# A third score tile shared by turns with pairs of row maxima, in the last four units of an attention block

## The chip, the cores and the metric

One core of one Trainium2 chip runs the whole kernel as one program. The metric is the time of one execution on the device in microseconds (us), median of several runs; a separate, profiled execution gives the trace.

## What is computed

An adaptive-LayerNorm transformer block on 2048 tokens of 448 channels: attention of 16 heads of 28 channels, and an MLP of 1792 hidden channels.

```python
mod = (_silu(c) @ w_mod).reshape(c.shape[0], 6, 1, -1)
sa, ca, ga, sb, cb, gb = (mod[:, 0], ...)
h = _layernorm(x) * (1 + ca) + sa
x = x + ga * _A_ref(h, A_wqkv, A_wo)    # softmax(q k^T / sqrt(28)) v, 16 heads, then @ wo
h = _layernorm(x) * (1 + cb) + sb
x = x + gb * _B_ref(h, B_w1, B_b1, B_w2, B_b2)   # layernorm, gelu(h @ w1 + b1) @ w2 + b2
```

## The kernel before

The program has three parts: LayerNorm, q, k and v projections with a first share of the row maxima (to 169 us), attention (169 to 831 us), and the MLP (831 us to the end).

**Attention** runs 16 *units* u = 4 g + qt, g a group of four heads and qt a block of 512 queries. A unit has 16 *steps* kt, one for each 128 keys, so there are 256 steps; step = 16 u + kt. A step computes the scores of four heads in two *halves* hf of two heads each. A half is a PSUM tile of two banks, 128 keys x (2 x 512) queries, filled by six matmuls: three terms (high and low parts of q and k) for each of its two heads (L1162). Each head sits in its own 32 rows of the array, half 0 in rows 0 to 63 and half 1 in rows 64 to 127. ACT takes exp of each half (L1167, into slots d and c), and TensorE then multiplies the exps of the step *before* with v (`av`, L1132, four matmuls, the "AV" of a step) into tile o. PE's program is thus: first half, second half, AV of the step before, next step.

**Row maxima.** The softmax needs the maximum of every row of scores before a unit begins; it enters the scores as one more row of q. So beside its own work each step computes some of the maxima of later units: one maximum is one matmul of 28 rows x 512 keys from tiles kh and qh into a bank (L466, `max_mm`) and one VectorE reduce of that bank (L471). They are taken from a queue `mxq`; `n_maxima` gives three or four a step. `emit_max` puts one or two behind the first terms of the first half, and the others behind the last term of the second half. `max_fin` reduces, transposes and writes them into q by DMAs (L502, L509, L512).

**PSUM** has eight banks. Tiles s0 and s1 (two banks each) take the two halves by turns, o one, m1 one, and m2 two buffers of one bank each; maxima go into m1, m2, m2 by turns. When no maximum is left (`three`, in unit 14), `third_tile` closes m2 and opens a third score tile s2 in its banks.

**Units' ends.** When AV of a unit's last step has been issued, in the first step of the next unit, `end_unit` copies o (ACT, L1101) and schedules tasks by steps from there: `t_den` (step + 0, SP DMA L880), `t_rec` (+ 1 where the projection follows: DVE reciprocal, SP DMAs L888 and L890), `t_split` (+ 4, GpSimd L895), `t_split2` (+ 5: DVE cast L905, GpSimd L906). Results of head groups 0 to 2 lie in DRAM. Where the group is the last one, `load_o` (L868, in step + 0, behind `t_den` on SP) loads them, four or six DMAs of 256 KB, and `t_wo(t)` in steps 8 to 11 of units 12 to 15 multiplies them with wo: the *projection steps*. Each has 9 or 12 matmuls L386 into a maximum's bank, an ACT copy L926 and a GpSimd add.

**LayerNorm 2 of the first 512 tokens** starts within attention: 14 stages on VectorE and GpSimd, one a step from `last0 - 12` (last0 = 240, unit 15's first step), and four chunks, one a step from last0 + 3. A chunk has four transposes L267 into a maximum's bank, an ACT cast L994, and a DVE subtract L996 (L998) that frees the bank.

Of the kernel before, what the change touches and what calls it, by code (L numbers as in the profile page):

```python
# [31 lines left out]
NTT = S // 128  # L32
P1RATE = 4
YTAGS = [f"{a}{i}" for a in ("kh", "qh") for i in range(4)]
EPS = 1e-5
# [4 lines left out]
def tile_adaln_block(ctx: ExitStack, tc: tile.TileContext, x, wqkv, wo, w1, b1, w2, b2, c, w_mod, out):  # L40
# [29 lines left out]
    def nm(t):  # L70
        uid[0] += 1
        return f"{t}_{uid[0]}"
# [10 lines left out]
    def slot4(tag, inner, dt=F32R):  # L83
# [4 lines left out]
        return lambda k: t2[k // 2][:, k % 2]  # L88

    def ps_s2():  # L90
        s_ring.append(s_ring.pop(0))
        key = s_ring[-1]
        return ps_pools[key][1].tile([128, 2, 512], F32, tag=key, name=nm(key), bufs=1)

# [380 lines left out]
    def pair_diff(g, qt, i, j):  # L475
# [12 lines left out]
        return rest  # L488

    def load_hi(kind, g, b):  # L490
        tg = ("kh" if kind else "qh") + str(b)
# [70 lines left out]

    last_j = [None]

    def emit_max(n, half=None):
        for _ in range(n):
            if not mxq:
                return
            fits = [x for x, m in enumerate(mxq[:32]) if half is None or (m[4] // 2 == half and m[4] != last_j[0])]
            g, qt, cch, i, j = mxq.pop(fits[0] if fits else 0)  # L570
            last_j[0] = j
            max_one(g, qt, cch, i, j)
            count(g, qt, [cch])


# [219 lines left out]
    for key in ("s0", "s1"):  # L795
        ps_open(key)
    s_ring[:] = ["s1", "s0"]
    mx_ring[:] = ["m1", "m2", "m2"]

    def third_tile(on):  # L800
        ps_close("m2" if on else "s2")
        ps_open("s2" if on else "m2", "right")
        s_ring[:] = s_ring + ["s2"] if on else ["s1", "s0"]
        mx_ring[:] = ["m1"] if on else ["m1", "m2", "m2"]

    phase1[0] = False
# [64 lines left out]
    def unit_end_tasks(u, o_sb):  # L871
# [184 lines left out]
    def at(step, fn):  # L1056
        sched.setdefault(step, []).append(fn)
# [49 lines left out]
    o = None  # L1107
    plain = [0]
    three = False


    def is_wo(s_):
        return s_ // NKT >= NU - NB and 8 <= s_ % NKT < 12

    def left_steps(s_):
        rest = range(s_, NKT * (NU - 1) - 6)
        n_wo = sum(is_wo(x) for x in rest)
        return len(rest) - n_wo, n_wo


    def n_maxima(s_):
        n_plain, n_wo = left_steps(s_)
        over = len(mxq) - 7 * n_plain // 2
        if is_wo(s_):
            return max(0, -(-over // max(n_wo, 1)))
        plain[0] += 1
        return 4 if plain[0] % 2 or (over > 3 * n_wo and over > 0) else 3

# [8 lines left out]
    ptags = (["d0", "c0", "c1"], ["c0h", "c1h"])  # L1137
    done_max = set()
    for u in range(NU):
        g, qt = divmod(u, NB)  # L1140
        for kt in range(NKT):
            step = u * NKT + kt
            if kt == 1 and u + 1 < NU and u + 1 not in qst:
                load_q(u + 1)
            if kt == NKT - 6 and u + 1 < NU:
                finish_max(*divmod(u + 1, NB))
            tick_late()
            if not (three or mxq or late):
                three = True
                third_tile(True)  # L1150
            pt = [slot(tags[step % len(tags)], [128, 2, 512], F32) for tags in ptags]
            n = n_maxima(step)
            n0 = 1 if n == 3 and step % 4 == 3 else 2

            ks, qs = kst[(g, kt // 4)], qst[u]
            kc = slice((kt % 4) * 128, (kt % 4 + 1) * 128)
            for hf in range(2):
                s2 = ps_s2()
                for term, (kp, qp) in enumerate(((0, 0), (1, 0), (0, 1))):
                    for jj in range(2):  # L1160
                        rows_ = slice(64 * hf + 32 * jj, 64 * hf + 32 * jj + DH + (term == 0))
                        pe.matmul(s2[:, jj, :], ks[rows_, kp, kc], qs[rows_, qp, :], start=(term == 0), stop=(term == 2))  # L1162
# [4 lines left out]
                act.activation(pt[hf], s2, AF.Exp, scale=SCALE)  # L1167
# [22 lines left out]


    third_tile(False)
    w_copy[0] = act.copy
    LAG = 2
# [102 lines left out]
```

## Time and profile before

| what | value |
|---|---|
| median of 3 runs | 1128.87 us (1128.83 to 1129.13) |
| profiled execution | 1130.08 us, span 1128.0 us |
| TensorE (PE) busy | 1116.4 us, 99% of the span |
| VectorE (DVE) | 843.7 us, 75% |
| ScalarE (ACT) | 672.0 us, 60% |
| GpSimd (POOL) | 209.6 us, 19% |
| granted TensorE clock | full in all 40 slices |
| DMA | 81.19 MB, 72 GB/s in the mean |

A matmul's end is modelled in the trace, its start is recorded. A step's length is therefore read from the start of its first score matmul to that of the next step. A row of the timeline has start, duration, engine, line, operation, tiles and, in brackets, the idle time of the engine ahead of it and what ended it.

### The profile page before, as it was taken

The page shows a single profiled execution, that of the slowest core. Times are in us where ns is not written, and L with a number is a line of the kernel's source. Part 1 is how long each engine was busy: PE and PEld are TensorE (multiplying, and loading weights), DVE is VectorE, ACT ScalarE, POOL GpSimd, SP SyncE. Part 2 cuts the span into 40 slices and gives each one's busy share as a digit, 9 for nine tenths or more (in the row PEclk, how much of TensorE's full clock was granted, in tenths as well). Part 3 has the DMA queues.
Part 4 walks back from the last instruction along what each step waited for, and adds up shares of the span by engine and source line. Part 5 has one row for each costly group of instructions (what it writes and reads, how often), then busy time and mean ns, then how long its engine had stood idle before and what let it go on. Part 6 is the DMA issues. An engine that isn't in the chain of part 4 may idle for free.

```text
span 1128.0 us, 20665 instructions
## 1 busy us (share of the span) xinstructions
PE 1116.4 (99%) x8319; PEld 670.1 (59%) x8319; DVE 843.7 (75%) x1485; ACT 672.0 (60%) x823; POOL 209.6 (19%) x211
## 2 busy tenths in 40 slices
PE   8999999999999999999999999999999999999998
PEld 6756674444444444444444454545468888888887
DVE  6968788999999999999999978595448853444322
ACT  4555657888887888788788867576752321111110
POOL 1533332110000000000000020217114504123000
PEclk9999999999999999999999999999999999999999
DMA  9562263121121211311111312020422100000000
GB/s 303 202 200 88 91 200 114 48 84 41 58 95 57 58 40 57 91 53 58 53 44 58 112 41 83 4 85 1 137 73 78 35 33 1 1 33 1 33 1 33
DMA packets 49341, 81.19 MB, mean 72 GB/s; under 512 B 12311, under 2 KB 18702, under 8 KB 49234
## 3 DMA queue, kind: packets, MB, share of 16 engines
q1 hardware_dynamic: 48762, 79.14, 22.1%
q8 instruction: 65, 1.06, 0.4%
q10 hardware_dynamic: 148, 0.46, 0.1%
q0 software_dynamic: 336, 0.28, 0.1%
q14 instruction: 30, 0.25, 0.1%
HBM read 55.04 MB, written 26.48 MB: 72 GB/s over the span
## 4 chain that ended last, share of the span: by engine, by line
PE 94%; DVE 3%; ACT 1%; DMA 1%; issue 1%; POOL 0%; SPq 0%; DVEq 0%; ACTq 0%; POOLq 0%
PE s L1162 26%; PE o L1132 22%; PE m L386 16%; PE pa L386 8%; PE m L466 6%; PE s L1232 3%; PE s L1233 3%; PE s L1231 3%; DVE mxp L471 2%; PE t L1232 1%; PE t L1233 1%; PE t L1231 1%; DMA slot_c<-in_w_mod_dram 1%; PE ma L466 1%; PE o L267 1%
## 5 line engine op out<-in xcount | busy, mean ns | idle before, releaser
L471 DVE TENSOR_REDUCE mxp<-m 128x1 f32<-128x512 f32 x884 | 568.8, 686 | 75.3 <-PE m L466 41.1
L1162 PE MATMUL s<-slot_b,slot_a 28*128 28x512 f32 (+1 forms) x3072 | 376.3, 420 | 0.0
L1162 PEld LDWEIGHTS s<-slot_b,slot_a 28*128 28x128 f32 (+1 forms) x3072 | 213.0, 184 | 247.4 <-ACT slot_c L1167 124.1
L466 PE MATMUL m<-kh,qh 28*128 28x512 f32 x863 | 287.6, 472 | 1.2 <-DVE mxp L471 0.9
L1167 ACT ACTIVATE slot_c<-s 128x1024 f32<-128x1024 f32 x170 | 174.3, 1025 | 75.9 <-PE s L1162 75.6
L1132 PE MATMUL o<-slot_c,v 128*32 128x512 f32 x680 | 178.8, 605 | 0.0
L1208 ACT ACTIVATE full<-m,b_col 128x512 f32<-128x512 f32 x56 | 38.6, 689 | 192.0 <-PE m L386 175.5
L1132 PE MATMUL o<-slot_c1h,v 128*32 128x512 f32 x512 | 134.7, 605 | 0.0
L1132 PE MATMUL o<-slot_c0h,v 128*32 128x512 f32 x512 | 134.7, 605 | 0.0
L1167 ACT ACTIVATE slot_c0h<-s 128x1024 f32<-128x1024 f32 x128 | 130.4, 1019 | 2.4 <-PE m L386 2.4
L1167 ACT ACTIVATE slot_c1h<-s 128x1024 f32<-128x1024 f32 x128 | 130.4, 1019 | 0.0
L1211 DVE CAST hi<-full 128x512 fp32r<-128x512 f32 x56 | 25.5, 455 | 134.6 <-ACT full L1208 134.6
L466 PEld LDWEIGHTS m<-kh,qh 28*128 28x128 f32 x863 | 114.3, 182 | 8.6 <-DVE mxp L471 5.1
L1167 ACT ACTIVATE slot_d<-s 128x1024 f32<-128x1024 f32 x86 | 88.1, 1025 | 39.3 <-PE s L1162 39.1
L895 POOL TENSOR_TENSOR osb<-osb,osb 128x512 f32<-128x512 f32 x16 | 20.9, 1307 | 441.1 <-DMA osb<-drec 356.8
L1132 PE MATMUL o<-slot_d,v 128*32 128x512 f32 x344 | 90.5, 605 | 0.4 <-ACT osb L1101 0.4
L386 PE MATMUL m<-y,slot_a 128*128 128x512 f32 x160 | 60.7, 395 | 0.0
L1132 PEld LDWEIGHTS o<-slot_c,v 128*32 128x32 f32 x680 | 24.5, 108 | 52.4 <-issue 49.5
L1212 DVE TENSOR_TENSOR lo<-full,hi 128x512 fp32r<-128x512 f32 x56 | 44.2, 788 | 5.9 <-DVE hi L1211 0.9
L471 DVE TENSOR_REDUCE mxp<-ma 128x1 f32<-128x512 f32 x54 | 35.6, 683 | 7.1 <-PE m L466 4.8
L386 PE MATMUL m<-y,slot_v 128*128 128x512 f32 x112 | 39.2, 396 | 0.0
L386 PE MATMUL m<-y,slot_b 128*128 128x512 f32 x112 | 39.0, 398 | 0.0
(316 smaller groups left out, 1626.7 us busy)
## 6 DMA issues: line engine op xcount, KB each, us to landing
slot_b<-d SPq DMA_DIRECT2D x32, 256.0 KB
slot_a<-d SPq DMA_DIRECT2D x32, 256.0 KB
d<-lo SPq DMA_DIRECT2D x28, 256.0 KB
d<-hi SPq DMA_DIRECT2D x16, 256.0 KB
osb<-drec SPq DMA_DIRECT2D x15, 256.0 KB
out_dram<-xn SPq DMA_DIRECT2D x16, 224.0 KB
raw<-in_B_w_dram SPq DMA_DIRECT2D x14, 224.0 KB
qh<-d SPq DMA_DIRECT2D x12, 256.0 KB
```

Of the source, the lines that this page charges most:

```text
L386: pe.matmul(p, a, b, start=(i == 0), stop=(i == len(terms) - 1))
L466: pe.matmul(m, qh_sb[(g, qt)][js, i * 128 : (i + 1) * 128], k[js, :], start=True, stop=True)
L471: dve.tensor_reduce(out=mxp[(g, qt)][:, i, j, cch : cch + 1], in_=m, op=ALU.max, axis=AX.X)
L1132: pe.matmul(o[32 * j : 32 * j + 32, :], v_sb[kt // 4][:, kt % 4, 4 * g + j, :], p[j // 2][:, j % 2, :], start=(kt == 0), stop=(kt == NKT - 1),
L1162: pe.matmul(s2[:, jj, :], ks[rows_, kp, kc], qs[rows_, qp, :], start=(term == 0), stop=(term == 2))
L1167: act.activation(pt[hf], s2, AF.Exp, scale=SCALE)
L1208: act.activation(gf, p, AF.Gelu_apprx_tanh, bias=b1_col[:, i : i + 1])
L1211: dve.tensor_copy(ghi, gf)
L1212: dve.tensor_tensor(out=glo, in0=gf, in1=f(ghi), op=ALU.subtract)
L1231: pe.matmul(pp, ghi[:, ts], w_hi, start=(m == 0), stop=False)
L1232: pe.matmul(pp, ghi[:, ts], w_lo, start=False, stop=False)
L1233: pe.matmul(pp, glo[:, ts], w_hi, start=False, stop=(m == NFT - 1))
```

## The change

From step 192 (`RING`), in steps that are no projection steps, m2 is closed and s2 open, so that there are three score tiles and one bank m1. The first half is always in s0, and the two halves swap their order with each step (`first`). The second half is in s1 in even steps and in s2 in odd ones (`turns`); the other of the two takes a *pair* of maxima, two matmuls and one reduce of both banks (`emit_pair`), which stands ahead of the second half's third term. One single maximum in m1 stands behind the first half's first term. That makes three a step; a fourth (`extra`) is planned for but is taken in no step. In projection steps m2 is opened again, and they take four maxima (`WO_MAX`) while there are any; the last are in step 235, before in step 233. `ready_max` picks only maxima whose tiles were loaded three steps ago. In steps below 192 there are four and three by turns, as before, from the same tiles, but picked in another order.

`load_o` leaves the tasks of a unit's end and is scheduled three steps ahead of it (steps 189, 205, 221 and 237). `load_q` is called at step 4 of a unit instead of 1, `finish_max` at step 12 instead of 10. Step 0 has two maxima fewer. LayerNorm 2's stages and chunks start four steps later, the chunks from last0 + 7, so that three of them fall into projection steps. The diff, cut to its core:

```diff
+LAST_MAX = NKT - 4
+RING = 192
+WO_MAX = 4
...
+    def emit_pair(half, t):
+        near = ready_max()
+        for a, m in enumerate(near):
+            n = m[:4] + (m[4] + 1,)
+            if m[4] == 2 * half and n in near:
...
+                for jj in range(2):
+                    max_mm(g, qt, i, j + jj, kh_sb[(g, cch)], lambda: t[:, jj])
+                dve.tensor_reduce(out=mxp[(g, qt)][:, i, j : j + 2, cch], in_=t, op=ALU.max, axis=AX.X)
...
-        if len(parts) > 1 and not staged:
-            tasks.append((0, lambda: load_o(qt)))
...
+    for u in range(NU - NB - 1, NU - 1):
+        at(NKT * (u + 1) - 3, lambda qt=u % NB: load_o(qt))
...
     for i in range(14):
-        at(last0 - 12 + i, lambda i=i: lnst[0][0](i))
+        at(last0 - 8 + i, lambda i=i: lnst[0][0](i))
     for k in range(NC):
-        at(last0 + 3 + k, lambda k=k: lnst[0][1](k))
+        at(last0 + 7 + k, lambda k=k: lnst[0][1](k))
...
-            if kt == 1 and u + 1 < NU and u + 1 not in qst:
+            if kt == 4 and u + 1 < NU and u + 1 not in qst:
                 load_q(u + 1)
-            if kt == NKT - 6 and u + 1 < NU:
+            clock[0] = step
+            if kt == LAST_MAX and u + 1 < NU:
                 finish_max(*divmod(u + 1, NB))
...
+            first = step % 2 if step >= RING else 0
...
+            was, ring = ring, step >= RING and (three or not is_wo(step))
+            if ring != was:
+                third_tile(ring)
...
+            n_max = 0 if ring else WO_MAX if is_wo(step) else 4 - step % 2
...
+            for n, hf in enumerate((first, 1 - first)):
+                s2 = ps_s2() if three else ps_two((now[0] if n else "s0") if ring else ("s0", "s1")[n])
                 for term, (kp, qp) in enumerate(((0, 0), (1, 0), (0, 1))):
+                    if ring and n == 1 and term == 2 and mxq:
+                        emit_pair(first, ps_two(turns[1 - step % 2]))
                     for jj in range(2):
                         rows_ = slice(64 * hf + 32 * jj, 64 * hf + 32 * jj + DH + (term == 0))
                         pe.matmul(s2[:, jj, :], ks[rows_, kp, kc], qs[rows_, qp, :], start=(term == 0), stop=(term == 2))
-                    if hf == 0 and term < min(n0, n):
-                        emit_max(1, 1)
-                    if hf == 1 and term == 2 and n > n0:
-                        emit_max(n - n0, 0)
+                    if n == 0 and term < n0 <= n_max:
+                        emit_single(1, ps_mx)
+                    if n == 1 and term == 2:
+                        for _ in range(n_max - n0):
+                            emit_single(0, ps_mx)
+                    if ring and (n, term) == ((1, 0) if late_one else (0, 0)) and not three:
+                        emit_single(1 - first, ps_mx)
...
             if step == 0:
                 v_task(NB - 1, 3, ps_mx())
-                emit_max(2)
```

The order of TensorE's instructions in a plain step of unit 12, step 206, before. An instruction's row has its line, the tile written and the tiles read, with numbers that count the tiles; the scores are s1 and s0, the maxima m1 and m2, AV is L1132.

```order
L1162 MATMUL s1_2226_9312<-slot_b0_1976_8251,slot_a3_2099_8772 128x512 x2
L466 MATMUL m1_2227_9315<-kh2_1789_7469,qh2_1681_7017 128x512
L1162 MATMUL s1_2226_9312<-slot_b0_1976_8251,slot_a3_2099_8772 128x512 x2
L466 MATMUL m2_2228_9320<-kh2_1789_7469,qh2_1681_7017 128x512
L1162 MATMUL s1_2226_9312<-slot_b0_1976_8251,slot_a3_2099_8772 128x512 x2
L1162 MATMUL s0_2229_9326<-slot_b0_1976_8251,slot_a3_2099_8772 128x512 x6
L466 MATMUL m2_2230_9333<-kh2_1789_7469,qh2_1681_7017 128x512
L466 MATMUL m1_2231_9336<-kh2_1789_7469,qh2_1681_7017 128x512
L1132 MATMUL o_2109_8811<-slot_c0_2217_9279,v3_231 32x512 x2
L1132 MATMUL o_2109_8811<-slot_c1h_2218_9280,v3_231 32x512 x2
```

The same step after the change, from its single maximum (two score matmuls into s0 stand ahead of it) to the pair of step 207.

```order
L471 MATMUL m1_2217_9307<-kh3_1780_7440,qh2_1723_7198 128x512
L1224 MATMUL s0_2216_9304<-slot_b0_1998_8346,slot_a3_2100_8773 128x512 x4
L1224 MATMUL s1_2218_9315<-slot_b0_1998_8346,slot_a3_2100_8773 128x512 x4
L471 MATMUL s2_2219_9320<-kh0_1864_7784,qh2_1723_7198 128x512 x2
L1224 MATMUL s1_2218_9315<-slot_b0_1998_8346,slot_a3_2100_8773 128x512 x2
L1183 MATMUL o_2108_8811<-slot_c1h_2206_9265,v3_231 32x512 x2
L1183 MATMUL o_2108_8811<-slot_c0_2205_9264,v3_231 32x512 x2
L1224 MATMUL s0_2222_9333<-slot_b0_1998_8346,slot_a3_2100_8773 128x512 x2
L471 MATMUL m1_2223_9336<-kh3_1780_7440,qh2_1723_7198 128x512
L1224 MATMUL s0_2222_9333<-slot_b0_1998_8346,slot_a3_2100_8773 128x512 x4
L1224 MATMUL s2_2224_9344<-slot_b0_1998_8346,slot_a3_2100_8773 128x512 x4
L471 MATMUL s1_2225_9349<-kh0_1864_7784,qh2_1723_7198 128x512 x2
```

The four maxima in one-bank tiles have become a single in m1 and a pair in s2 (in s1 in the next step), and the second half is in the other of the two.

TensorE in unit 15, a chunk's step before, from the scores of step 244 to the next scores.

```order
L1162 MATMUL s1_2551_10734<-slot_b1_2389_10027,slot_a1_2035_8499 128x512 x6
L1162 MATMUL s0_2552_10742<-slot_b1_2389_10027,slot_a1_2035_8499 128x512 x6
L1132 MATMUL o_2520_10625<-slot_d0_2537_10696,v0_228 32x512 x2
L1132 MATMUL o_2520_10625<-slot_c1h_2538_10697,v0_228 32x512 x2
L267 MATMUL m1_2553_10754<-ident_1_77,xn_2464_10325 128x128
L267 MATMUL m1_2553_10754<-ident_1_77,xn_2474_10376 128x128
L267 MATMUL m1_2553_10754<-ident_1_77,xn_2483_10422 128x128
L267 MATMUL m1_2553_10754<-ident_1_77,xn_2492_10477 128x128
L1162 MATMUL s2_2556_10763<-slot_b1_2389_10027,slot_a1_2035_8499 128x512 x6
```

After, step 249, from its scores to the first projection matmuls.

```order
L1224 MATMUL s0_2550_10851<-slot_b1_2381_10079,slot_a2_2065_8627 128x512 x6
L1224 MATMUL s2_2551_10859<-slot_b1_2381_10079,slot_a2_2065_8627 128x512 x6
L1183 MATMUL o_2487_10578<-slot_c1_2540_10800,v2_230 32x512 x2
L1183 MATMUL o_2487_10578<-slot_c0h_2541_10801,v2_230 32x512 x2
L272 MATMUL m1_2552_10871<-ident_1_77,xn_2459_10450 128x128
L272 MATMUL m1_2552_10871<-ident_1_77,xn_2468_10491 128x128
L272 MATMUL m1_2552_10871<-ident_1_77,xn_2475_10521 128x128
L272 MATMUL m1_2552_10871<-ident_1_77,xn_2481_10550 128x128
L391 MATMUL m1_2553_10878<-slot_e0_489_2037,slot_a2h_2465_10482 128x448
L391 MATMUL m1_2553_10878<-slot_e1_490_2038,slot_a2h_2465_10482 128x448
L391 MATMUL m1_2553_10878<-slot_e0_489_2037,slot_a2h_2465_10482 128x448
```

The transposes L272 are followed by L391 into the next tile of the same bank, m1, where before scores of the next step stood.

SP's queue at the end of unit 12, from its den DMA to the broadcast of the reciprocal, before.

```order
L880 DMA den_2257_9446<-osb_2247_9409 128x1x16
L868 DMA slot_a2h_2258_9448<-o00_2039 128x512
L868 DMA slot_a2h_2258_9448<-o10_2042 128x512
L868 DMA slot_a3h_2259_9451<-o01_2040 128x512
L868 DMA slot_a3h_2259_9451<-o11_2043 128x512
L868 DMA slot_b1h_2260_9454<-o02_2041 128x512
L868 DMA slot_b1h_2260_9454<-o12_2044 128x512
L888 DMA drec_2269_9492<-den_2257_9446 128x16
L890 DMA osb_2270_9494<-drec_2269_9492 128x1x512
```

After:

```order
L914 DMA slot_a2h_2211_9293<-o00_2039 128x512
L914 DMA slot_a2h_2211_9293<-o10_2042 128x512
L914 DMA slot_a3h_2212_9296<-o01_2040 128x512
L914 DMA slot_a3h_2212_9296<-o11_2043 128x512
L914 DMA slot_b1h_2213_9299<-o02_2041 128x512
L914 DMA slot_b1h_2213_9299<-o12_2044 128x512
L926 DMA den_2240_9421<-osb_2232_9389 128x1x16
L934 DMA drec_2248_9454<-den_2240_9421 128x16
L936 DMA osb_2249_9456<-drec_2248_9454 128x1x512
```

The six loads stand ahead of den, and den, drec and the broadcast to osb follow one another.

More of the change, by code (lines that the diff above doesn't have):

```diff
@@ L88, in slot4, with ps_two @@
         return lambda k: t2[k // 2][:, k % 2]
+    def ps_two(key):
+        return ps_pools[key][1].tile([128, 2, 512], F32, tag=key, name=nm(key), bufs=1)
     def ps_s2():
         s_ring.append(s_ring.pop(0))
[L92 to L93 removed]
+        return ps_two(s_ring[-1])
     def ps_s():
@@ L488, in pair_diff @@
         return rest
+    loaded = {}
+    clock = [0]
     def load_hi(kind, g, b):
+        loaded[(kind, g, b)] = clock[0] + 3
         tg = ("kh" if kind else "qh") + str(b)
@@ L1107, in tile_adaln_block @@
     o = None
-    plain = [0]
+    due = [0.0]
+    now = [None]
     three = False
@@ L1113, in is_wo, with extra @@
         return s_ // NKT >= NU - NB and 8 <= s_ % NKT < 12
[L1115 to L1123, printed above, removed]
-        if is_wo(s_):
-            return max(0, -(-over // max(n_wo, 1)))
-        plain[0] += 1
-        return 4 if plain[0] % 2 or (over > 3 * n_wo and over > 0) else 3
+    def extra(s_):
+        if is_wo(s_):
+            return False
+        most = 0
+        need = 0
+        for v in range(s_ // NKT + 1, NU):
+            need += left.get(divmod(v, NB), 64)
+            rest = range(s_, NKT * (v - 1) + LAST_MAX)
+            n_wo = sum(is_wo(x) for x in rest)
+            n_plain = len(rest) - n_wo
+            if n_plain > 0:
+                most = max(most, (need - 3 * n_plain - WO_MAX * n_wo) / n_plain)
+        due[0] += min(most, 1)
+        if due[0] < 1:
+            return False
+        due[0] -= 1
+        return True
     def av(u, kt, p, o):
@@ L1137, in tile_adaln_block @@
     ptags = (["d0", "c0", "c1"], ["c0h", "c1h"])
-    done_max = set()
+    after = False
+    ring = False
     for u in range(NU):
```

55 lines of the change are left out of this document (41 added, 14 removed).

## The prediction, made before the changed kernel ran

> **What bounds the kernel now.** I read the page's first and fifth parts, then the score matmuls by stretches of steps, then the timeline of a few steps.
>
> ```profile
> span 1128.0 us, 20665 instructions
> PE 1116.4 (99%) x8319; PEld 670.1 (59%) x8319; DVE 843.7 (75%) x1485; ACT 672.0 (60%) x823; POOL 209.6 (19%) x211
> L471 DVE TENSOR_REDUCE mxp<-m 128x1 f32<-128x512 f32 x884 | 568.8, 686 | 75.3 <-PE m L466 41.1
> ```
>
> TensorE is never idle for long, but "busy" includes matmuls that wait half-way through a step. The length of a step tells more. These rows hold the score matmuls of L1162 alone; each stretch runs from the first score matmul of a step to that of another, 12 records a step, so x96 is 8 steps and x48 is 4. The columns are window and length, PE, PEld, clock, DMA share and GB/s.
>
> ```profile
> 642.00:661.60 19.60, 12.14 (x96) 6.90 (x96) 1.00 0.38 123
> 661.60:678.80 17.20, 5.43 (x48) 3.11 (x48) 1.00 0.00 1
> 708.20:728.60 20.40, 5.81 (x48) 3.19 (x48) 1.00 0.01 2
> 738.40:758.80 20.40, 12.11 (x96) 6.83 (x96) 1.00 0.37 118
> 758.80:778.10 19.30, 5.00 (x48) 2.73 (x48) 1.00 0.01 1
> 778.10:786.10 8.00, 4.30 (x48) 2.47 (x48) 1.00 0.00 0
> 786.10:804.50 18.40, 8.19 (x96) 4.56 (x96) 1.00 0.46 143
> 804.50:823.90 19.40, 4.08 (x48) 2.26 (x48) 1.00 0.31 88
> ```
>
> A plain step of units 12 to 14 takes 19.60/8 = 2.45 us, four of them 9.80; with no maxima left and three score tiles it takes 8.00/4 = 2.00. So maxima cost 0.45 a step. A projection step takes 17.20/4 = 4.30 (nine matmuls), 5.10 (unit 13) and about 4.8 (twelve matmuls). The timeline shows the two kinds of plain step, four maxima from 656.76 and three from 659.51.
>
> ```profile
> 656.76 0.49 PE L1162 MATMUL s<-slot_b,slot_a 29*128 29x512 f32 x2
> 656.77 0.51 PE L466 MATMUL m<-kh,qh 28*128 28x512 f32 x2
> 657.34 2.58 DVE L471 TENSOR_REDUCE mxp<-m 128x1 f32<-128x512 f32 x4 [0.17 <-PE m L466]
> 657.58 0.18 PEld L1162 LDWEIGHTS s<-slot_b,slot_a 29*128 29x128 f32 x2 [0.29 <-ACT slot_c1h L1167]
> 657.60 0.50 PE L466 MATMUL m<-kh,qh 28*128 28x512 f32 x1
> 657.77 1.03 ACT L1167 ACTIVATE slot_d<-s 128x1024 f32<-128x1024 f32 x1 [0.24 <-PE s L1162]
> 657.92 0.40 PE L1162 MATMUL s<-slot_b,slot_a 28*128 28x512 f32 x2
> 658.08 0.50 PE L466 MATMUL m<-kh,qh 28*128 28x512 f32 x1
> 658.51 0.62 PE L1132 MATMUL o<-slot_c,v 128*32 128x512 f32 x2
> 659.51 0.50 PE L1162 MATMUL s<-slot_b,slot_a 29*128 29x512 f32 x2
> 659.76 0.74 PE L1162 MATMUL s<-slot_b,slot_a 29*128 29x512 f32 x8
> 660.30 0.41 PE L466 MATMUL m<-kh,qh 28*128 28x512 f32 x2
> 660.67 0.62 PE L1132 MATMUL o<-slot_d,v 128*32 128x512 f32 x2
> 661.66 0.50 PE L1162 MATMUL s<-slot_b,slot_a 29*128 29x512 f32 x2
> 666.42 0.49 PE L1162 MATMUL s<-slot_b,slot_a 29*128 29x512 f32 x2
> ```
>
> With S for a step's first score matmul: the step of four is 659.51 - 656.76 = 2.75 long with its AV matmuls (L1132) at S+1.75; the step of three is 2.15 long with AV at S+1.16; AV to the next S takes 0.99 to 1.00 in both. The difference, 0.59, has two causes that end at the same time. The fourth maximum's buffer is free when the first one's reduce (0.69 us, begun 0.57 behind its matmul) is done. And the second half's weights wait for ACT at 657.58: with two score tiles the exp of the half before, second in ACT's queue, frees its tile only at S+0.82. A third tile takes away the latter.
>
> **The plain steps from 192 on.** Of the 48 steps from 192 to 239, 32 plain ones become ring steps with three maxima: a single in m1 and a pair in the tile that the step's second half leaves free. A reduce of 1024 elements is not in the trace. Its nearest rows are the 0.686 of 512 elements above and
>
> ```profile
> L502 DVE TENSOR_REDUCE m<-mxp 128x16 fp32r<-128x64 f32 x16 | 3.5, 220 | 0.6
> ```
>
> The slope is (686 - 220)/448 = 1.04 ns an element, so 1024 elements take 686 + 512 x 1.04 = 1.22 us; twice 0.686 = 1.37 is the upper bound, and 0.69 the lower. I take 1.22. The Trainium skill, "VectorE: DVE Perf Modes", section on the TRN2 errata, gives (120 + elements)/0.96 GHz, which is an estimate of 1.19 us; by it the sum below would be 0.4 us less.
>
> Three chains could set a ring step. First, tile s0 is the first half's in each step: matmuls to exp 657.77 - 656.76 = 1.01, exp 1.03, release 0.05 (estimate), together 2.09. Second, TensorE itself: the step of three, 1.16 + 0.99 = 2.15, holds as many matmuls. Third, the pair. Its matmuls use the first half's row groups, which are done with three terms by 660.30 - 659.51 = S+0.79. They end some 0.46 later, when the single's reduce (S+0.58 to S+1.27) is done as well. The pair's reduce runs to S+2.49. Only then can the next step's second half start in that tile, at S+2.54; from the second half's first term to AV is 660.67 - 659.76 = 0.91, and to the step after that 0.99. That is 4.44 for two steps, 2.22 a step. I take 2.22 as the longest; with 1.37 for the reduce it would be 2.29.
>
> Before, these 32 steps took 8 x 2.45 in unit 12 and as much in unit 13, 4 x 2.45 behind the projection steps of either, and 20.40 in unit 14: 79.2. After: 29 at 2.22, three at 2.15 that follow a projection step, and 0.6 for exps that wait behind ACT's copy at a unit's end: 71.4. On entering a projection step the two m2 buffers wait for the exp in s2 (S+0.8), but the fourth maximum holds that step to S+1.74 anyway; 0.1 each, 0.3. **-7.5 us.** Steps below 192 issue as many maxima in the same tiles as before, in another order: nothing, cover being the 13 steps between a key tile's load and its first use, of which at least 3 stay; 0.59 a step if one had to wait.
>
> **Projection steps.** The maxima that the ring no longer takes go into steps 200-203, 216-219 and 232-235, four each and three in step 235. At 0.59 for a fourth, unit 12's last three go from (17.20 - 4.76)/3 = 4.15 to 4.75, and its first, 666.42 - 661.66 = 4.76, is as long as with four already, by ACT: 19.0. Unit 13's 20.40 contain a wait of about 1.1 on VectorE for GpSimd:
>
> ```profile
> 694.74 0.91 SPq L868 DMA_DIRECT2D slot_b1h<-o  x2
> 696.94 0.32 SPq L888 DMA_DIRECT2D drec<-den  x1
> 701.56 0.55 SPq L890 DMA_DIRECT2D osb<-drec  x1
> 706.59 1.29 POOL L895 TENSOR_TENSOR osb<-osb,osb 128x512 f32<-128x512 f32 x1 [25.80 <-DMA osb<-drec]
> 707.92 0.43 DVE L905 CAST hi<-osb 128x512 fp32r<-128x512 f32 x1 [1.12 <-POOL osb L895]
> ```
>
> The reciprocal's two small DMAs lie 4.62 us apart behind the loads of L868 and end late; the cast L905 waits 1.12 with reduces queued behind it. The early load removes that: (20.40 - 1.1 - 0.2)/4 = 4.78, +0.59 = 5.37, times four 21.5. Unit 14 had 3, 2, 0 and 0 maxima and now has 4, 4, 4, 3: 3 x 5.37 + 4.78 = 20.9. Sum 61.4 against 17.20 + 20.40 + 19.30 = 56.9. **+4.5 us.** The statistics of the second LayerNorm fall into these steps too, but VectorE's four reduces leave 2.6 us of each free. The load's DMAs queue on SP three steps ahead of the unit's end, ahead of a den that isn't ready. Steps 236-239 have no maxima in either: 8.1 against 8.0.
>
> **Unit 15.** The chunk (four transposes L267 into m1, ACT cast L994, DVE subtract L996) moves from steps 243-246 to 247-250, and in 248-250 the projection matmuls ask for the same m1 directly behind it.
>
> ```profile
> 795.18 0.98 PE L1162 MATMUL s<-slot_b,slot_a 29*128 29x512 f32 x12
> 797.09 0.66 PE L267 MATMUL m<-ident,xn 128*128 128x128 f32 x4
> 797.10 1.02 ACT L1167 ACTIVATE slot_c0h<-s 128x1024 f32<-128x1024 f32 x1
> 798.00 0.59 ACT L994 CAST y<-m 128x512 fp32r<-128x512 f32 x1
> 798.63 0.69 DVE L996 TENSOR_TENSOR y<-m,y 128x512 fp32r<-128x512 f32 x1 [1.98 <-ACT y L994]
> 797.67 0.99 PE L1162 MATMUL s<-slot_b,slot_a 29*128 29x512 f32 x12
> 809.97 0.47 PE L386 MATMUL m<-slot_e,lo 128*128 128x448 f32 x1 [0.79 <-POOL lo L906]
> 810.37 0.99 PE L1162 MATMUL s<-slot_b,slot_a 29*128 29x512 f32 x12
> ```
>
> A chunk step is 797.67 - 795.18 = 2.49. The cast stands behind both exps, and m1 is free at 798.63 + 0.69 + 0.05, S+4.19, while the transposes end at S+2.5. Step 248 begins 5.8 ahead of 810.37 and loses 1.2 by the late cast; the other three take (19.40 - 5.8)/3, about 4.55, of which 1.9 lie ahead of the twelve projection matmuls, so these take 2.65. Begun at S+4.19, they make a step of 6.84. Unit 15's first twelve, with 18.40 - 4 x 2.5 - 2.0 = 6.4 for its first three: 6.4 + 4 x 1.98 + 2.5 + 3 x 6.84 + 4.55 = 41.9 against 18.40 + 19.40 = 37.8, where the early load has taken the 1.2 us ahead of 809.97 away. **+4.1 us**; +5.3 if that wait stays, -2.8 if m1 is not waited for.
>
> **Step 0** has two maxima fewer, with reduces of 0.69: between 0 and -1.4, I take **-0.9**.
>
> **Sum:** -7.5 + 4.5 + 0.1 + 4.1 - 0.9 = +0.3 us on the profiled execution's 1130.08 (span 1128.0), which is 1.2 above the median 1128.87. On the median: 1129.1. About 0.2%, 2.3 us, is what a measurement of this kernel can tell from no change.
>
> **Rivals.** *The ring at its floor* (faster): the pair's reduce overlaps better or takes nearer its lower bound, and a ring step runs at TensorE's 2.15, or s0's 2.09. Then 29 x (0.07 to 0.13) = 2 to 4 us less; a projection step whose reduces lie under its own matmuls gives up to 2 more: 1123.5 to 1126.8, around 1125.4. For it: DVE has 0.67 + 1.22 = 1.9 of work for 2.2. Against it: the pair's chain is serial through both engines.
>
> *The pair holds the score tile* (slower): the second half waits for the reduce and ACT, fed late, hands s0 back late too. It decides when the pair's reduce ends later than S+2.5. With 1.37 a step is 2.29 (+2.0); if the single's reduce comes first and the pair waits behind another DVE job as well (0.43, a cast like L905), 2.4 or more: +2.3 to +7, around 1133.
>
> *Matmuls in program order* (slower): in the rows above the third maximum starts at 657.60, ahead of score terms at 657.92, though it stands behind all twelve in the program. If no matmul could pass another, the second half would follow the first's three terms, the pair would stand ahead of its last term, AV would come at S+1.46, and 29 x 0.23 gives +7: 1136. The Trainium skill, "TensorE: Matmul & The Clock Gate", section on row/col tiling, says that matmuls are strictly first in, first out in start and end; the rows speak against it.
>
> *The early load does nothing* (slower, small): GpSimd is late for another reason; +1.1 + 1.2: 1131.4.
>
> **How the numbers follow.** Forecast as summed, by itself 1126.6 to 1131.6: 0.42. Ring at its floor: 0.28. Tile held: 0.20. Program order: 0.04. Load in vain: 0.06. With an error of 2.5 us in either direction a third of the forecast's case lies outside 1126.6 to 1131.1, 0.08 below and 0.07 above; the load in vain counts as slower. Faster 0.28 + 0.08 = 0.36, same 0.27 and slower 0.20 + 0.04 + 0.06 + 0.07 = 0.37. The range, 1123.5 to 1135.0, leaves out the program order and the far ends of the first two rivals.
>
> **What would show it.** Right: ring steps of 2.22, pair reduces of 1.22 with next to no idle time of DVE between single and pair, projection steps of 4.75 and 5.37, L391's first matmul waiting 1.7 us for L1040 in steps 248-250, and no wait for GpSimd in steps 216 and 248. Wrong: ring steps at 2.45 or 2.09, or m1 free by S+2.5.

## The result, and the profile after

The changed kernel takes 1133.41 us in the median of 6 runs (1133.27 to 1135.35), the kernel before 1129.0 (1127.95 to 1132.12): a ratio of 1.0041, 95% interval 1.003 to 1.0052: 0.4% slower, and the two ranges don't meet. The profiled execution took 1133.55 us, 3.5 more than that of before; the spans differ by 3.8. The point forecast was 1129.1; the range, to 1135.0, holds the result.

From the page of the changed kernel, and from its groups by form the row of the new reduce:

```profile
span 1131.8 us, 20637 instructions
PE 1113.8 (98%) x8319; PEld 667.6 (59%) x8319; DVE 840.3 (74%) x1453; ACT 671.9 (59%) x823; POOL 209.6 (19%) x211
L476 DVE TENSOR_REDUCE mxp<-m 128x1 f32<-128x512 f32 x820 | 528.2, 685 | 85.8 <-PE m L471 53.4
```
```profile
L615 DVE TENSOR_REDUCE mxp<-s 128x2 f32<-128x1024 f32 x32 | 39.2, 1225 | 1.4
```

The 32 pairs have replaced 64 single reduces, VectorE is busy 3.4 us less and PE 2.6 less, in a longer span: no engine has more work, so the time went into waits. Where, the score matmuls (now L1224) by stretches tell; the columns are as in the prediction, and the stretches are the same steps, 192-199, 200-203, 216-219, 224-231, 232-235, 236-239, 240-247 and 248-251:

```profile
642.44:660.75 18.31, 10.90 (x96) 6.46 (x96) 1.00 0.29 84
660.75:680.44 19.69, 5.54 (x48) 3.12 (x48) 1.00 0.01 2
707.36:729.40 22.04, 5.54 (x49) 3.13 (x49) 1.00 0.01 2
738.34:756.25 17.91, 10.50 (x96) 6.35 (x96) 1.00 0.31 94
756.25:777.82 21.57, 5.53 (x48) 3.11 (x48) 1.00 0.00 1
777.82:785.80 7.98, 4.08 (x48) 2.27 (x48) 1.00 0.44 133
785.80:802.81 17.01, 8.44 (x98) 4.88 (x98) 1.00 0.40 124
802.81:827.86 25.05, 3.92 (x48) 2.09 (x48) 1.00 0.17 47
```

Summed from the starts of all steps' score matmuls, against the terms of the prediction (us):

| steps | before | after | difference | forecast |
|---|---|---|---|---|
| the 32 ring steps | 79.14 | 72.08 | -7.06 | -7.5 |
| the 12 projection steps 200 to 235 | 56.91 | 63.30 | +6.39 | +4.5 |
| 236 to 239 | 8.02 | 7.98 | -0.04 | +0.1 |
| 240 to 251 | 37.85 | 42.06 | +4.21 | +4.1 |
| 0 and 1 | 8.13 | 7.46 | -0.67 | -0.9 |
| 2 to 191 | 464.72 | 465.49 | +0.77 | 0 |

The rows sum to +3.6. The other 0.2 us of the spans lie outside them, ahead of step 0 above all, whose start varies between 168.9 and 170.2 us over the traces of the changed kernel and its variants. The forecast's -7.5 for the ring holds +0.3 for entering the projection steps, a wait that the table counts with these: -7.8 and +4.8 is the comparison by steps.

What the ring saves, the projection steps beside it give back; what remains is unit 15. Two stretches of the timeline show how. First two ring steps of unit 13, from 693.93 and from 696.14, with S for a step's first score matmul as before:

```profile
693.93 0.50 PE L1224 MATMUL s<-slot_b,slot_a 29*128 29x512 f32 x2
694.51 0.69 DVE L476 TENSOR_REDUCE mxp<-m 128x1 f32<-128x512 f32 x1 [0.36 <-PE s L1224]
694.70 0.19 PEld L471 LDWEIGHTS s<-kh,qh 28*128 28x128 f32 x2 [0.20 <-ACT slot_c1h L1234]
694.74 0.47 PE L471 MATMUL s<-kh,qh 28*128 28x512 f32 x2
695.25 1.23 DVE L615 TENSOR_REDUCE mxp<-s 128x2 f32<-128x1024 f32 x1
696.14 0.49 PE L1224 MATMUL s<-slot_b,slot_a 29*128 29x512 f32 x2
696.47 0.79 PE L1224 MATMUL s<-slot_b,slot_a 28*128 28x512 f32 x8
697.43 0.62 PE L1183 MATMUL o<-slot_d,v 128*32 128x512 f32 x2
```

The pair's matmuls start at S+0.81, its reduce at S+1.32 behind the single's, and it ends at 696.48, when the next step's remaining scores start; AV follows 0.95 later. The steps are 2.21 and 2.29 long. The pair's weights (the PEld row) wait 0.20 us for ACT's exp into slot_c1h, which reads the scores that were in the pair's tile before; the prediction's three chains don't have this wait. Then step 248, a chunk with the projection behind it:

```profile
802.81 0.98 PE L1224 MATMUL s<-slot_b,slot_a 29*128 29x512 f32 x12
804.72 0.66 PE L272 MATMUL m<-ident,xn 128*128 128x128 f32 x4
805.64 0.59 ACT L1038 CAST y<-m 128x512 fp32r<-128x512 f32 x1
806.27 0.69 DVE L1040 TENSOR_TENSOR y<-m,y 128x512 fp32r<-128x512 f32 x1 [0.88 <-ACT y L1038]
807.01 0.88 PE L391 MATMUL m<-slot_e,slot_a2h 128*128 128x448 f32 x3 [1.64 <-DVE y L1040]
809.66 0.72 PE L1224 MATMUL s<-slot_b,slot_a 29*128 29x512 f32 x5
```

TensorE stands idle for 1.64 us until m1 is free, at S+4.20, and the step is 6.85 long.

### The profile page after: what moved, and what is told of

The parts are those of the page before. It is cut to its first block, busy times and chain, and to the rows that moved or that the text cites. A ratio compares the mean times of both kernels' runs of the same rounds, so it can differ in the third digit from the quotient of the medians.

```text
span 1131.8 us, 20637 instructions
## 1 busy us (share of the span) xinstructions
PE 1113.8 (98%) x8319; PEld 667.6 (59%) x8319; DVE 840.3 (74%) x1453; ACT 671.9 (59%) x823; POOL 209.6 (19%) x211
## 3 DMA queue, kind: packets, MB, share of 16 engines
q1 hardware_dynamic: 48762, 79.14, 22.5%
## 4 chain that ended last, share of the span: by engine, by line
PE 93%; DVE 3%; ACT 2%; issue 1%; DMA 1%; SPq 0%; DVEq 0%; ACTq 0%
PE s L1224 25%; PE o L1183 22%; PE m L391 16%; PE pa L391 8%; PE m L471 6%; PE s L1299 3%; PE s L1300 3%; PE s L1298 3%; DVE mxp L476 2%; PE t L1299 1%; PE t L1300 1%; PE t L1298 1%; DMA slot_c<-in_w_mod_dram 1%; PE o L272 1%; PE ma L471 1%
## 5 line engine op out<-in xcount | busy, mean ns | idle before, releaser
L476 DVE TENSOR_REDUCE mxp<-m 128x1 f32<-128x512 f32 x820 | 528.2, 685 | 85.8 <-PE m L471 53.4
L1224 PE MATMUL s<-slot_b,slot_a 28*128 28x512 f32 (+1 forms) x3072 | 370.6, 420 | 1.0 <-ACT v L453 0.6
L1224 PEld LDWEIGHTS s<-slot_b,slot_a 28*128 28x128 f32 (+1 forms) x3072 | 211.3, 184 | 245.3 <-ACT slot_c L1234 126.0
L471 PE MATMUL m<-kh,qh 28*128 28x512 f32 x799 | 272.6, 471 | 2.1 <-DVE mxp L476 1.4
L471 PEld LDWEIGHTS m<-kh,qh 28*128 28x128 f32 x799 | 108.7, 182 | 12.0 <-DVE mxp L476 7.3
L391 PE MATMUL m<-y,slot_a 128*128 128x512 f32 x160 | 60.7, 395 | 0.0
L615 DVE TENSOR_REDUCE mxp<-s 128x2 f32<-128x1024 f32 x32 | 39.2, 1225 | 1.4
L391 PE MATMUL m<-y,slot_v 128*128 128x512 f32 x112 | 39.2, 396 | 0.0
```

Source lines behind the costliest of these rows:

```text
L391: pe.matmul(p, a, b, start=(i == 0), stop=(i == len(terms) - 1))
L471: pe.matmul(m, qh_sb[(g, qt)][js, i * 128 : (i + 1) * 128], k[js, :], start=True, stop=True)
L476: dve.tensor_reduce(out=mxp[(g, qt)][:, i, j, cch : cch + 1], in_=m, op=ALU.max, axis=AX.X)
L615: dve.tensor_reduce(out=mxp[(g, qt)][:, i, j : j + 2, cch], in_=t, op=ALU.max, axis=AX.X)
```

## The experiments

### Unit 15: the chunks ahead of the projection steps

```diff
-        at(last0 - 8 + i, lambda i=i: lnst[0][0](i))
+        at(last0 - 9 + i, lambda i=i: lnst[0][0](i))
...
-        at(last0 + 7 + k, lambda k=k: lnst[0][1](k))
+        at(last0 + 4 + k, lambda k=k: lnst[0][1](k))
```

> The changed kernel with the LayerNorm 2 stages one step earlier (from step 231) and the four chunks in steps 244 to 247, ahead of the projection steps of unit 15. Theory (the chunk and the projection matmuls contend for bank m1): steps 248 to 250 fall from 6.84 to about 4.55 us, 3 x 2.29 = 6.9 less; steps 244 to 247 grow to 2.5 each, 2.0 to 1.5 more in all. Net -5.4, about 1128.0 us, level with the kernel before or 0.1% below it. Rival (the stall only moves: step 248 then waits for GpSimd's lo, as before the change): 1.2 of it comes back and the time is about 1129.2. Rival (steps 248 to 250 are long for another reason, the hi and lo of unit 14): they stay at 6.8 and nothing changes, 1133.4.

1129.02 us, ratio to the kernel before 1.000 (0.999 to 1.001). Steps 248 to 251 fall from 25.06 to 18.18, steps 240 to 247 rise from 17.00 to 18.45: -5.43 against -5.4. Step 248 is 4.55, so nothing took the place of the stall there (step 232 is 0.34 longer, 5.95). Without the contention for m1 the whole of the loss that can be measured is gone.

### Projection steps: which rows the maxima use

```diff
-            first = step % 2 if step >= RING else 0
+            first = step % 2 if step >= RING and (three or not is_wo(step)) else 0
```

> The changed kernel with half 0 first in all projection steps, so that the maxima placed in the first half use the other half's rows of the array. In the trace of the changed kernel odd projection steps (201, 203, 217, 219, 233) have AV at S+1.93 to 1.95 and their first maximum starts 0.33 behind S, even ones (202, 218, 234) have S+1.74 and 0.01. Theory (in odd steps half 1 stands first and the maxima share its rows): odd steps fall by 0.2 to AV at S+1.74, six of them, -1.2 us, about 1132.2. Rival (odd steps are late because of the bank that the projection of the step before leaves behind): no change, 1133.4, odd steps still at 1.94.

1133.09 us, 1.0032 (1.0021 to 1.0044); the median is 0.3 below the changed kernel's, less than the expected 1.2; the trace is 1.0 shorter up to step 255. In the changed kernel, step 201 (from 665.74) and step 202 (from 670.70):

```profile
665.74 0.72 PE L1224 MATMUL s<-slot_b,slot_a 29*128 29x512 f32 x5
666.08 0.39 PE L471 MATMUL m<-kh,qh 28*128 28x512 f32 x1
667.67 0.62 PE L1183 MATMUL o<-slot_c,v 128*32 128x512 f32 x2
670.70 0.50 PE L1224 MATMUL s<-slot_b,slot_a 29*128 29x512 f32 x2
670.71 0.50 PE L471 MATMUL m<-kh,qh 28*128 28x512 f32 x2
672.45 0.62 PE L1183 MATMUL o<-slot_c1h,v 128*32 128x512 f32 x2
```

And step 201 of this variant:

```profile
665.08 0.50 PE L1224 MATMUL s<-slot_b,slot_a 29*128 29x512 f32 x2
665.09 0.51 PE L471 MATMUL m<-kh,qh 28*128 28x512 f32 x2
666.83 0.62 PE L1183 MATMUL o<-slot_c,v 128*32 128x512 f32 x2
```

In odd projection steps the change puts half 1 first and still takes the first maxima from half 1, whose rows it shares: they start 0.34 behind S instead of 0.01. With half 0 first, steps 201, 203, 217, 219 and 233 fall from 4.96, 4.97, 5.57, 5.58 and 5.58 to 4.77, 4.76, 5.39, 5.38 and 5.39. Shown in the trace, 0.2 a step.

### What the ring is worth

```diff
-WO_MAX = 4
+WO_MAX = 3
...
-            first = step % 2 if step >= RING else 0
+            first = step % 2 if three else 0
...
-            was, ring = ring, step >= RING and (three or not is_wo(step))
+            was, ring = ring, three
```

> The changed kernel without the ring: m2 stays open until the last maximum, four and three maxima by turns in plain steps and three in projection steps, as before the change, so that the early load, the later LayerNorm 2 and the new picking order are left of the change. Theory (the ring's gain of 7.1 us in plain steps is paid back by 6.4 us in projection steps): plain steps from 192 on return to 2.45, projection steps to 4.15 and 4.77, and the sum is within 1 us of the changed kernel's: about 1133, with steps 248 to 250 at 6.84 still. Rival (the ring itself makes it slower): about 1129.

1133.59 us, 1.0032 (1.0019 to 1.0045). Plain steps return to 2.45 (78.31 for the 32, +6.2), projection steps to 57.39 (-5.9), and steps 248 to 251 stay at 25.05. With its heavier projection steps the ring is 0.3 us ahead in these two traces, which shows no gain: the trace without it lost 0.8 us in step 200 (5.53; 4.74 in the kernel before with the early load alone, below), where VectorE's cast waited 1.44 us for a late reciprocal.

### Where the surplus maxima are cheaper

```diff
-WO_MAX = 4
+WO_MAX = 3
```

> The changed kernel with three maxima instead of four in projection steps; ten ring steps take a fourth one in m1. Theory (a projection step pays 0.6 to 0.8 for its fourth maximum, a ring step less, since VectorE has 0.3 of 2.24 us free and the next step's pair takes up part of the rest): projection steps return to 4.15 and 4.77, 7.3 us less in all, ring steps with a fourth cost 0.35 more, +3.5; net -3.8, about 1129.6. Rival (the ring is bound by VectorE, a fourth reduce costs its full 0.69 and shifts the pair): +6.9, net -0.4, about 1133.

1137.5 us, 1.0067 (1.0054 to 1.0079): neither. Projection steps fall by 5.8 to 57.52, but ring steps rise by 9.6 to 81.69, 0.87 for each of the fourth maxima (there are eleven, not ten), more than a whole reduce. Ten of the steps with a fourth take 2.73 to 2.83 and one, step 204, 3.45; those behind them take 2.2 to 2.6. About 2 us of the 9.6 lie in steps 204 and 220, the first behind projection steps (3.45 and 2.88, in the changed kernel 2.17 both); in step 204 the single waits for ACT's copy of the projection out of a maximum's bank. The rest is still more than the 5.8 saved. The expectation, that VectorE's free 0.3 us would take up half, is refuted; the projection step is the cheaper place.

### The pair's reduce in two

```diff
-                dve.tensor_reduce(out=mxp[(g, qt)][:, i, j : j + 2, cch], in_=t, op=ALU.max, axis=AX.X)
+                for jj in range(2):
+                    dve.tensor_reduce(out=mxp[(g, qt)][:, i, j + jj, cch : cch + 1], in_=t[:, jj], op=ALU.max, axis=AX.X)
```

> The changed kernel with each pair's reduce of 1024 elements (1.23 us in its trace) as two of 512 (2 x 0.69 = 1.38), so that the pair holds its score tile 0.15 longer and nothing else moves. Theory (a ring step of 2.24 is set by the chain pair matmuls, reduce, next step's second half, which takes two steps): 0.075 a step, 32 steps, +2.4 us, ring steps of about 2.31, about 1135.8. Rival (TensorE's own work or tile s0 sets the ring step): no change, 1133.4 and 2.24. Rival (VectorE's sum, 0.69 + 1.38 + 0.69 of waiting, sets it): +0.15 a step, +4.8.

1134.13 us, 1.0043 (1.003 to 1.0056). Ring steps rise by 0.61 in all, 0.02 a step. The expectation was mis-sized: back-to-back reduces overlap, two take 1.29, only 0.06 more than one of 1.23. So the run decides nothing between 0.03 a step and none.

### The pair's reduce cut to half

```diff
-                dve.tensor_reduce(out=mxp[(g, qt)][:, i, j : j + 2, cch], in_=t, op=ALU.max, axis=AX.X)
+                dve.tensor_reduce(out=mxp[(g, qt)][:, i, j : j + 2, cch], in_=t[:, :, :256], op=ALU.max, axis=AX.X)
...
+        dve.tensor_scalar(out=m32[:, 0:16], in0=f(m32)[:, 0:16], scalar1=-212.0, scalar2=None, op0=ALU.add)
```

> The changed kernel with each pair's reduce over only the first 256 of 512 keys of either bank (the other keys' maxima are left out, and a margin of 212 is subtracted from the maxima of a unit by one small VectorE instruction), so a pair's reduce takes 0.69 instead of 1.23 us and nothing else moves. Splitting the pair's reduce had lengthened it by only 0.06 (two back to back take 1.29), so that it told little. Theory (pair matmuls, reduce and next second half set two ring steps: 1.32 + 1.23 + 0.05 + 0.95 + 0.99 = 4.5 in the trace): it falls to 4.0, TensorE's 2.15 takes over, ring steps 2.15, -0.09 x 29 = -2.6, about 1130.8. Rival (TensorE or tile s0 sets 2.24 already): no change, 1133.4.

1134.4 us, 1.0039 (1.0025 to 1.0054). The ring steps take 71.44 instead of 72.08: -0.64 against -2.6. (Steps below 192 are 1.3 longer here; the added instruction is the only other edit.) The steps now alternate between about 2.14 and 2.29, and its timeline, from a step's S at 701.73 (2.14 long) and the next one's at 703.87 (2.29 long), shows what holds the longer ones:

```profile
701.73 0.50 PE L1225 MATMUL s<-slot_b,slot_a 29*128 29x512 f32 x2
702.73 1.02 ACT L1235 ACTIVATE slot_d<-s 128x1024 f32<-128x1024 f32 x1 [0.35 <-PE s L1225]
703.65 1.02 ACT L1235 ACTIVATE slot_c1h<-s 128x1024 f32<-128x1024 f32 x1
703.87 0.50 PE L1225 MATMUL s<-slot_b,slot_a 29*128 29x512 f32 x2
703.90 0.95 PE L1225 MATMUL s<-slot_b,slot_a 29*128 29x512 f32 x8
704.73 0.18 PEld L471 LDWEIGHTS s<-kh,qh 28*128 28x128 f32 x2 [0.32 <-ACT slot_c1h L1235]
705.17 0.62 PE L1184 MATMUL o<-slot_c1h,v 128*32 128x512 f32 x2
705.27 0.69 DVE L616 TENSOR_REDUCE mxp<-s 128x2 f32<-128x512 f32 x1
706.16 0.50 PE L1225 MATMUL s<-slot_b,slot_a 29*128 29x512 f32 x2
```

At 703.87 both halves' scores start at once, and the pair waits: its tile held the second half of the step before, and ACT reads that until 704.67. The third score terms and AV stand behind the pair. So two chains have nearly the same length. Through the reduce, two steps take 1.32 + 1.23 + 0.95 + 0.99 = 4.49, 2.25 each. Through ACT, counted from 701.73, the first half's exp starts at S+1.00, both exps end 1.94 later, the pair follows 0.06 behind, AV 0.44 and the next S 0.99 behind it: 4.43, 2.22 each. Shortening the first leaves the second. The second is read from this timeline; no run shortens it.

### The early load undone, in the changed kernel

```diff
-    for u in range(NU - NB - 1, NU - 1):
-        at(NKT * (u + 1) - 3, lambda qt=u % NB: load_o(qt))
...
+        if len(parts) > 1 and not staged:
+            tasks.append((0, lambda: load_o(qt)))
```

> The changed kernel with the stored results loaded where they were before the change, behind den on SP. Theory (the loads delay the reciprocal by 3 us, and the cast behind it holds VectorE): in unit 13 the wait was 1.1 us before the change; the ring's steps are 1.6 us shorter by then, so the wait grows to about 2.7, and about 2.5 of it reaches step 215 or 216; units 12 and 14 have 0.5 to 1 each; in unit 15 the 1.2 us is hidden behind m1. Sum +3 to +4.5, about 1137. Rival (what the early load saves is what it saved before, independent of the ring): +1.1, 1134.5. Rival (nothing): 1133.4.

1152.23 us, 1.0204 (1.0191 to 1.0218): the direction of the theory, four times its size. Steps 200, 216, 232 and 248 grow by 0.8, 5.5, 4.8 and 5.8. From step 216's timeline, and from its windows, where the clock stands ahead of the last two figures (PE, PEld, DVE, ACT, POOL, clock, DMA share, GB/s):

```profile
710.29 1.26 POOL L941 TENSOR_TENSOR osb<-osb,osb 128x512 f32<-128x512 f32 x1 [26.42 <-DMA osb<-drec]
711.59 0.43 DVE L951 CAST hi<-osb 128x512 fp32r<-128x512 f32 x1 [4.71 <-POOL osb L941]
711.93 0.68 DVE L476 TENSOR_REDUCE mxp<-m 128x1 f32<-128x512 f32 x1
712.66 0.50 PE L471 MATMUL m<-kh,qh 28*128 28x512 f32 x1 [3.33 <-DVE mxp L476]
```
```profile
713.00:716.00 3.00, 2.60 (x22) 1.04 (x16) 2.68 (x5) 1.74 (x2) 0.36 (x1) 0.69 0.00 0
716.00:718.00 2.00, 2.00 (x12) 0.95 (x5) 0.55 (x1) 0.30 (x1) 0.00 (x0) 0.62 0.00 0
```

The cast waits for GpSimd for 4.71 us at the head of VectorE's queue, the reduces behind it don't free their banks, and TensorE stands idle for 3.33 us. Then its granted clock falls: in windows of 1 us from 713 it is 1.00, 0.56, 0.50, 0.50, 0.73 and 1.00. The expectation had a wait of 2.7, by steps that are 1.6 us shorter. Those came (1.65), but counted from step 208 GpSimd's add is also 1.5 us later than before the change, 19.4 instead of 17.9: SP issues the broadcast 5.94 us behind drec instead of 4.62, and the add follows 6.18 us behind that instead of 5.04.

### LayerNorm 2 four steps later, in the kernel before

```diff
-        at(last0 - 12 + i, lambda i=i: lnst[0][0](i))
+        at(last0 - 8 + i, lambda i=i: lnst[0][0](i))
...
-        at(last0 + 3 + k, lambda k=k: lnst[0][1](k))
+        at(last0 + 7 + k, lambda k=k: lnst[0][1](k))
```

> The kernel before with only LayerNorm 2's stages and chunks four steps later, as in the change. Theory: steps 248 to 250 grow from 4.55 to 6.84, steps 243 to 246 fall from 2.5 to 2.0; the 1.2 us that step 248 lost to GpSimd are hidden behind m1; unit 15 +4.2, and step 230 loses its statistics on VectorE, -0.9: +3.3, about 1132.3. Rival (the stall of 248 adds to the wait for GpSimd, and projection steps 232 to 235 wait for VectorE's statistics): +5 or more.

1138.41 us, 1.008 (1.0066 to 1.0095): +9.2, which is the rival's "+5 or more", by the first of its two reasons; steps 232 to 235 are as before. Step 230 does lose its 0.87, and 249 and 250 are 6.88 and 6.84, but step 248 is 13.35. Its timeline and a window:

```profile
806.62 1.26 POOL L895 TENSOR_TENSOR osb<-osb,osb 128x512 f32<-128x512 f32 x1 [10.51 <-DMA osb<-drec]
807.91 0.43 DVE L905 CAST hi<-osb 128x512 fp32r<-128x512 f32 x1 [6.56 <-POOL osb L895]
808.26 0.68 DVE L996 TENSOR_TENSOR y<-m,y 128x512 fp32r<-128x512 f32 x1
809.00 0.68 PE L267 MATMUL m<-ident,xn 128*128 128x128 f32 x4 [4.18 <-DVE y L996]
```
```profile
811.00:812.50 1.50, 1.08 (x3) 1.00 (x4) 1.39 (x3) 0.00 (x0) 0.00 (x0) 0.50 0.43 106
```

The chunk's subtract L996 of step 247 now stands behind the late cast on VectorE and keeps m1, so step 248's transposes wait 4.18 us; then they wait for each other as in the change, at half the clock. The reciprocal is no later than before the change (POOL at 806.62 against 806.71). So the two parts belong together: in this kernel the later LayerNorm 2 needs the early load.

### The early load alone

```diff
-        if len(parts) > 1 and not staged:
-            tasks.append((0, lambda: load_o(qt)))
...
+    for u in range(NU - NB - 1, NU - 1):
+        at(NKT * (u + 1) - 3, lambda qt=u % NB: load_o(qt))
```

> The kernel before with only the stored results loaded three steps ahead of a unit's end. Theory (the loads delayed the reciprocal): the wait of 1.1 us in step 216 and that of 1.2 us in step 248 go, -2.3, about 1126.8. Rival (a step later something else holds them, as the ring's own first projection steps show): half of it, 1128.

1128.09 us, 0.9986 (0.9977 to 0.9995), 0.1% faster. In the trace step 216 falls from 6.08 to 5.37 and step 248 from 5.79 to 4.71: -1.8, between the two. Step 216 keeps AV at S+1.73, as the first projection step of unit 12 has it without such a wait.

### The changed kernel mended

The chunks ahead and half 0 first in projection steps, both edits from above:

> The changed kernel with both mended: the chunks in steps 244 to 247, and half 0 first in projection steps. Theory: the two gains of 5.4 and 1.3 us add up, about 1126.7, 0.2% below the kernel before. Rival (a part of one is hidden in the other): 1128.

1128.39 us, 0.9998 (0.9989 to 1.0007), above the theory. Step 201 takes 4.77 and steps 248 to 251 take 18.18, as wanted, but step 200 is 6.45 in this execution instead of 4.98. From SP's queue and VectorE's in this run, then SP's in the run with half 0 first alone:

```profile
649.98 0.31 SPq L934 DMA_DIRECT2D drec<-den  x1
653.23 0.55 SPq L936 DMA_DIRECT2D osb<-drec  x1
660.70 0.43 DVE L951 CAST hi<-osb 128x512 fp32r<-128x512 f32 x1 [1.79 <-POOL osb L941]
```
```profile
649.47 0.31 SPq L934 DMA_DIRECT2D drec<-den  x1
650.87 0.55 SPq L936 DMA_DIRECT2D osb<-drec  x1
```

From the reciprocal's write (drec) to its broadcast SP took 3.25 us here and 1.40 there, from the same code. So even with the early load a slow DMA stops VectorE. The ring, which has made the steps ahead of the cast shorter, isn't needed for that: in the run without the ring the two lie 3.37 us apart, its cast waits 1.44 and step 200 takes 5.53. In the kernel before with the early load alone 3.19 us cost next to nothing (a wait of 0.10, step 200 4.74). There GpSimd's add started 5.2 us behind the broadcast's issue, in these two runs 6.2 and 6.4. In units 12 to 14 it is 4.9 to 5.6 us in the kernel before and its variants, and 5.9 to 6.6 in the changed kernel and its variants, where the two DMAs of `load_q`, moved to step 4, stand directly behind the broadcast on SP. Whether they delay it was not tried. The cast one step later, besides:

```diff
-        times = (0, 4, 8, 9) if staged else (0, 1, 4, 5)
+        times = (0, 4, 8, 9) if staged else (0, 1, 4, 6)
```

> The changed kernel with the chunks ahead of the projection steps, half 0 first in these, and VectorE's cast hi one step later, so that a late reciprocal no longer holds the reduces of a ring step. In the traces of the version without the last edit the reciprocal's second DMA came 1.7 us later in one execution than in another, and step 200 lost 1.5 us by it. Theory: step 200 always 4.98, about 1126.5 and a smaller spread of the times. Rival (lo is now late for the first projection step): +0.5 to 1 in each of steps 200, 216, 232 and 248, about 1129.

1128.28 us, 0.9988 (0.998 to 0.9997). Step 200 is 4.97 and the spread is 1127.65 to 1129.09, against 1127.2 to 1132.5 without the later cast, as the theory wants (the trace itself has the write in 1.40 us and tests nothing); but step 232 is 6.11 instead of 5.77 and step 248 is 5.11 instead of 4.55, which is the rival in two of four places, with 0.3 and 0.6. And the kernel before with the early load and the later cast:

> The kernel before with the early load and the cast one step later, without ring and with LayerNorm 2 where it was. Theory: as with the early load alone, about 1126.8, since no ring shortens the steps ahead of the cast; level with the mended changed kernel, so that the ring is worth nothing over it. Rival (the ring's gain of 7 us is worth more than its 6 in projection steps): 0.5 to 1 us above the mended one.

1128.04 us, 0.9989 (0.998 to 0.9997). Level with the mended one, so the ring is worth nothing that can be measured over the early load alone. Three runs lie about 0.1% below the kernel before: the early load alone, that with the later cast, and the mended changed kernel with the later cast.

## Why the prediction was right or wrong, point by point

- **The sum.** The trace has +3.8 us (spans) where it said +0.3; the sign that it put at 0.37 came. By steps, the miss is 1.6 us in projection steps, 0.8 in steps below 192, 0.7 in ring steps and 0.2 in steps 0 and 1, all to one side. That the range holds 1133.4 is luck: the forecast's own case ended at 1131.6, and the range reaches further only for a rival that did not happen as described (last point).
- **Ring steps**, 2.22 forecast, 2.25 measured; the reduce of 1024 elements takes 1.225 against the estimate of 1.22, and the chain through it is as reckoned. But "three chains could set a ring step" was incomplete: the pair's tile is also released by ACT, a fourth chain of 2.22. The two are nearly equal, so the size came out right, and halving the reduce did not bring the faster rival's floor.
- **Projection steps**, +4.5 forecast, +6.39 measured: the mis-sized term. A fourth maximum costs 0.59 only where the first maxima run in the other half's rows. The step "four each ... at 0.59 for a fourth" took all projection steps for alike; odd ones cost 0.2 more by their rows (five of them, 1.0 us, shown by putting half 0 first), and the first of each unit, 4.98, 5.60 and 5.57 with that mended, is 0.2 above the others. That this last 0.2 is the two m2 buffers' wait for the exp in s2, taken as 0.1, was not tried by itself. Step 235 takes 5.00 instead of 4.78, in either order of the halves; its cause stays open.
- **Unit 15**, +4.1 forecast, +4.21 measured, step 248 6.84 forecast and 6.85 measured. Right as to mechanism and size: moving the chunks took all of it back.
- **The early load**, 1.1 and 1.2 us forecast, 0.7 and 1.1 measured alone. What was not seen is that the change as a whole needs it: without it the same kernel is 19 us slower. The prediction priced the load against the old steps only.
- **Steps below 192** cost 0.77, not 0: three waits, 0.32 in step 60 and 0.2 in steps 89 and 161, of the kind that was priced "0.59 a step if one had to wait". That the new order in which maxima are picked causes them was not tried.
- **Steps 0 and 1**: -0.67 against -0.9, by two reduces fewer.
- **The rivals.** "The pair holds the score tile" gave the time closest to the result (1133), but for a reason that did not occur: ring steps did not reach 2.29 in the mean. Program order is refuted again: with matmuls unable to pass, ring steps would be 2.45. "The early load does nothing" is refuted by undoing it.

## What to carry to other kernels

Where two users of one bank are moved into the same step, work out when the first one's last reader is done: here ACT's cast and VectorE's subtract made each of three steps 2.3 us longer, and moving them out of the way took back the whole loss. A gain in one kind of step has to be set against where the displaced work goes (-7.1 against +6.4 us). And shorter steps take slack from every latency that spans steps: a wait of 1.1 us in front of an in-order queue became 4.7, about half of it by shorter steps and half by slower DMAs, and the step behind it grew by 5.5.

## What the runs showed of the hardware

An idle TensorE lost its clock here, but not each time. Idle times of 1.62 to 1.66 us, in steps 248 to 250 of the changed kernel and seven other runs, left the granted clock at 1.00. In the run with the early load undone, 3.33 us ahead of 712.66 brought it to 0.50, 1.4 us after the matmuls had resumed; in the same run 1.80 us ahead of 765.57 were enough (1.00 up to 765, 0.66 in the next us, then 0.50 up to 768 and beyond). In the run with LayerNorm 2 later it was 0.50 from 810 to 816 behind a wait of 4.18, and three matmuls L386 took 1.32 us together instead of 0.78. The Trainium skill, "TensorE: Matmul & The Clock Gate", section on the HAM clock gate, states that the clock falls to half after an idle window of about 3.4 us. The half agrees with these runs; the 1.80 us are less than such a window, so here less idling was enough once, and what else decided is not shown.

Reduces of 512 elements out of PSUM, 0.69 us each alone, overlap in a row: two take 1.29 (the pair's reduce in two), four 2.58 (the kernel before, at 657.34).
